# Decoding float64 weights on the chip: clearing the sign on ScalarE, and two decodes in every unit of the second stage

## The chip, the core and the metric

One core of a Trainium2 chip runs the whole program. The metric is the device time of one execution in microseconds (us). TensorE does the matrix products, VectorE and ScalarE the elementwise work and all reads of TensorE's output (PSUM), POOL (GpSimd) elementwise work between SBUF tiles, and SP issues the transfers. In views of the profile they are PE, DVE, ACT, POOL and SP; PEld is TensorE's loading of weights.

## What is computed

```python
def reference(**kwargs):
    ...
    attn_out = _attn_ref(**attn_kwargs)      # local causal attention plus a memory term, 4 x 8 heads, 576 x 64
    x = np.ascontiguousarray(attn_out.transpose(0, 2, 1, 3)).reshape(B * S, H * D)   # 2304 x 512
    x = _moe_ref(x=x, **moe_kwargs)
    return _moe2_ref(x=x, **moe2_kwargs)

def _moe_ref(x, w_in, w_out):                # 512 -> 2048 -> 512
    h = x @ w_in
    sp = np.where(h > 20.0, h, np.log1p(np.exp(np.minimum(h, 20.0))))
    g = h * np.tanh(sp)
    return (g @ w_out).astype(np.float32)

def _moe2_ref(x, w1, w2, w3, w_out):         # 512 -> 1024 -> 512
    a = x @ w1
    b = x @ w2
    h = a * b @ w3
    return (h @ w_out).astype(np.float32)
```

The weights come as float64, so each number is two 32-bit words in memory. The kernel builds each value out of the words and splits it into a rounded part and a remainder, for three products in place of one.

## The kernel before

The program has three stages. **Attention** goes over 16 pairs of heads. The **second stage** is `_moe_ref`: the 2048 hidden columns come in four quarters, and each quarter goes over eight units (four batches, `b`, by two halves, `z`, of 288 rows). In a unit `emit_h` makes the hidden values: 48 matmuls, then tanh, arctan and sine on ScalarE with two loads of its function table (L471, L474), a product on VectorE (L482), and the split into `gh` (ScalarE, L485) and `gl` (VectorE, L65). `emit_x2` multiplies them with the second weights: 48 matmuls into X banks of PSUM, which VectorE empties into `x2` (L575 in the first quarter, L577 later). It runs one unit behind `emit_h`. The **third stage** is `_moe2_ref`; w3 and the last weights are multiplied with each other (`fold`) during the last quarter and the start of the third stage.

`decode` turns a block of 128 x 512 weights into floats: a transfer of the raw words (`draw`, L92), six operations on VectorE (L98 to L104) and an addition on POOL (L105). `split_w` then rounds and subtracts on POOL into the weight tile `wqt` (L62, L65). `split_to_dram`, used by `predecode` for the weights of the third stage, does the same in place (L62, L120) and writes both parts to DRAM (L121, L122). The buffers `da`, `de` and `draw` exist once in attention and twice in the second stage, so a decode can't start until POOL, or a write, is done with an earlier one.

What is decoded when is set by generators: `steps(gen, n)` takes n blocks from one. Attention takes ten blocks. In the second stage `nextq` loads the eight blocks of the next quarter and `pre` the 22 blocks of the third stage that are left. The framework then orders each engine's instructions by its own simulated schedule, so their order is not that of the code; an engine works off its instructions in the order given to it.

Of the kernel before, what the change touches and what calls it, by code (L numbers as in the profile page):

```python
# [9 lines left out]
F32 = mybir.dt.float32  # L10
# [3 lines left out]
AF = mybir.ActivationFunctionType  # L14
ALU = mybir.AluOpType
# [6 lines left out]
def fused_kernel(ctx: ExitStack, tc, q, k, v, M_prev, z_prev, beta, w_in, w_out, w1, w2, w3, w_out2, out):  # L22
    nc = tc.nc
# [31 lines left out]
    def f(ap):  # L55
        return ap.bitcast(F32)
# [13 lines left out]
    def steps(gen, n):  # L70

        for _ in range(n):
            next(gen, None)
# [9 lines left out]
    def decoder(stack, raw, n):  # L83
        dec.update(pool=stack.enter_context(tc.tile_pool(name="dec", bufs=1)), raw=raw, n=n)

    def dec_tile(tag):
        return dec["pool"].tile([128, WN], F32, tag=tag, name=tag, bufs=dec["n"])

    def decode(src):

        r = dec["pool"].tile([128, WN, 2], I32, tag="draw", name="draw", bufs=dec["raw"])
        dm(out=r.rearrange("p n t -> p (n t)"), in_=src)  # L92
        lw, hw = r[:, :, 0], r[:, :, 1]
        a = dec_tile("da")
        e = dec_tile("de")
        ai, ei = a.bitcast(I32), e.bitcast(I32)
        V = nc.vector
        V.tensor_scalar(out=ai, in0=hw, scalar1=0x7FFFFFFF, scalar2=None, op0=ALU.bitwise_and)  # L98
        V.tensor_scalar(out=a, in0=a, scalar1=2.0 ** -15, scalar2=122879.9921875, op0=ALU.max, op1=ALU.min)  # L99
        V.tensor_scalar(out=ai, in0=ai, scalar1=3, scalar2=0x3FFFFFF8,  # L100
                        op0=ALU.logical_shift_left, op1=ALU.bitwise_and)
        V.scalar_tensor_tensor(out=ai, in0=hw, scalar=-0x40000000, in1=ai, op0=ALU.bitwise_and, op1=ALU.bitwise_or)  # L102
        V.tensor_scalar(out=ei, in0=ai, scalar1=-0x800000, scalar2=None, op0=ALU.bitwise_and)  # L103
        V.scalar_tensor_tensor(out=e, in0=lw.bitcast(U32), scalar=2.0 ** -52, in1=e, op0=ALU.mult, op1=ALU.mult)  # L104
        nc.gpsimd.tensor_tensor(out=a, in0=a, in1=e, op=ALU.add)  # L105
        return a, e
# [4 lines left out]
    def split_w(hi, lo, src):  # L111
        a, _ = decode(src)
        pool_round(hi, a)
        sub(lo, a, hi, nc.gpsimd)

    def split_to_dram(dst, src):

        a, e = decode(src)
        pool_round(e.bitcast(F32R), a)
        nc.gpsimd.tensor_tensor(out=a.bitcast(F32R), in0=a, in1=e, op=ALU.subtract)  # L120
        dm(out=dst[0], in_=e)  # L121
        dm(out=dst[1], in_=a)  # L122
# [16 lines left out]
    def predecode():  # L139
        for w, wd in ((w1, w1_dram), (w2, w2_dram), (w_out2, o2_dram)):  # L140
            for c in range(w.shape[0] // 128):
                for h in range(w.shape[1] // WN):
                    split_to_dram(wd[:, 128 * c:128 * c + 128, WN * h:WN * h + WN], words(w, 128 * c, WN * h))
                    yield
# [13 lines left out]
    def load_quarter(g):  # L158
        t = (wq if g % 2 == 0 else w2q[0]).tile([128, 2, KD + KQ, FQ], F32R, tag=f"wq{g % 2}", name="wqt")
        wts[g] = t  # L160
        for c in range(KD):
            split_w(t[:, 0, c], t[:, 1, c], words(w_in, 128 * c, FQ * g))
            yield
        for c in range(KQ):
            split_w(t[:, 0, KD + c], t[:, 1, KD + c], words(w_out, FQ * g + 128 * c, 0))
            yield
# [16 lines left out]
        out=mask, in_=mask, pattern=[[-1, 512]], compare_op=ALU.is_ge,  # L183
# [4 lines left out]
    for hv in (UP, DN):  # L188
        nc.gpsimd.affine_select(
            out=mask4[hv], in_=mask4[hv], pattern=[[-1, CH]], compare_op=ALU.is_ge,  # L190
# [263 lines left out]
    def emit_h(u):  # L454

        g, b, z = u
        t = wts[g]
        x = xl[b]
        cs = slice(CH * z, CH * z + CH)
        y = [wps[0].tile([128, 2, CH], F32, tag=f"y{i}", name="y", bufs=1) for i in range(2)]  # L460
        hp = []
        for m in range(KQ):
            o = bank(HU.get(u, HT[g == NQ - 1])[m])[:, 0:CH]
            ms = slice(128 * m, 128 * m + 128)
            for kk in range(KD):
                mm(o, t[:, 0, kk, ms], x[:, 0, kk, cs], kk == 0, False)
                mm(o, t[:, 0, kk, ms], x[:, 1, kk, cs], False, False)
                mm(o, t[:, 1, kk, ms], x[:, 0, kk, cs], False, kk == KD - 1)
            hp.append(o)
        for m in range(KQ):  # L470
            nc.scalar.activation(out=y[m // 2][:, m % 2], in_=hp[m], func=AF.Tanh, scale=0.5)  # L471

        d = wps[0].tile([128, 1], F32, tag="dum", name="dum", bufs=2)
        first = nc.scalar.activation(out=d, in_=y[1][:, 1, 0:1], func=AF.Sin, scale=0.0)  # L474
        with tc.issue_after(first.ins):
            for i in range(2):
                nc.scalar.activation(out=y[i], in_=y[i], func=AF.Arctan, scale=-0.5, bias=half)
        gg = []
        for i in range(2):
            nc.scalar.activation(out=y[i], in_=y[i], func=AF.Sin, scale=-2.0, bias=halfpi)  # L480
            for j in range(2):
                nc.vector.tensor_tensor(out=y[i][:, j], in0=y[i][:, j], in1=hp[2 * i + j], op=ALU.mult)  # L482
            gh = wps[0].tile([128, 2, CH], F32R, tag="gh", name="gh", bufs=3)
            gl = wps[0].tile([128, 2, CH], F32R, tag="gl", name="gl", bufs=3)
            nc.scalar.copy(out=gh, in_=y[i])  # L485
            sub(gl, y[i], gh)
            gg.append((gh, gl))
        gt[u] = gg
# [9 lines left out]
    pre = predecode()  # L498
# [61 lines left out]
    def emit_x2(u):  # L560
        g, b, z = u
        t = wts[g]
        gg = gt.pop(u)
        c0 = S * b + CH * z
        for m in range(KD):
            o = psX()[:, 0:CH]
            ms = slice(128 * m, 128 * m + 128)
            for kk in range(KQ):
                gh, gl = (x[:, kk % 2] for x in gg[kk // 2])
                mm(o, t[:, 0, KD + kk, ms], gh, kk == 0, False)  # L570
                mm(o, t[:, 1, KD + kk, ms], gh, False, False)
                mm(o, t[:, 0, KD + kk, ms], gl, False, kk == KQ - 1)
            d = x2[:, m, c0:c0 + CH]
            if g == 0:
                nc.vector.tensor_copy(out=d, in_=o)  # L575
            else:
                nc.vector.tensor_tensor(out=d, in0=d, in1=o, op=ALU.add)  # L577
# [37 lines left out]
    def from_dram(t, d, cols):  # L615
        for i in range(2):
            dm(out=f(t[:, i]), in_=d[i, :, cols].rearrange("(k p) f -> p k f", p=128))

    def w_slot(s, name):
        return xp.tile([128, 2, KD, 512], F32R, tag=f"xs{s}", name=name, padded_shape=[128, 2, KD, S])  # L620

    folding = fold()
    nextq = iter(())
    prev = None
    w1t, w2t, wft = [None, None], [None, None], [None]
    for u in [(g, b, z) for g in range(NQ) for b in range(B) for z in range(2)]:
        g, b, z = u
        last = g == NQ - 1
        if u not in gt:
            if last and fpool[0] is None:  # L630
                steps(nextq, 100)
                steps(pre, 100)
                dk.close()
                fpool[0] = fk.enter_context(tc.tile_pool(name="fp", bufs=1))
                decoder(fk, 1, 2)
            emit_h(u)
        if last:
            if z == 0 and b > 0:
                wt, wd = ((w1t, w1_dram), (w2t, w2_dram))[(b - 1) % 2]
                i = (b - 1) // 2  # L640
                wt[i] = w_slot(b - 1, "w12t")
                from_dram(wt[i], wd, slice(512 * i, 512 * i + 512))
            if b > 0:
                steps(folding, 3)
        if prev is not None:
            emit_x2(prev)
        if not last:
            if b == 0 and z == 0:
                nextq = load_quarter(g + 1)
            steps(nextq, 2)  # L650
            steps(pre, 1)
        prev = u
    emit_x2(prev)
    w2t[1] = w_slot(3, "w12t")
# [53 lines left out]
    for c in range(NC):  # L708
        emit_ab(c)
        if c == 1:  # L710
# [4 lines left out]
            for i in range(2):  # L715
                for s in range(2):
                    dm(
                        out=f(wft[0][:, i, 4 * s:4 * s + 4]),
                        in_=w_dram[i, 512 * s:512 * s + 512, :].rearrange("(k p) f -> p k f", p=128),
# [36 lines left out]
```

## Time and profile before

| | |
|---|---|
| median of the runs before | 1073.4 us (1073.21 to 1075.92, 3 runs) |
| the profiled execution | 1075.49 us, with a span of 1073.7 us from the first to the last instruction |
| TensorE, matmuls | 1023.7 us busy, 95% of the span |
| VectorE | 671.9 us, 63% |
| ScalarE | 548.0 us, 51% |
| POOL | 387.3 us, 36% |
| granted TensorE clock | 0.991 of full speed on average |
| attention, second stage, third stage | about 0 to 285 us, 285 to 720 us, the rest; they overlap at the ends |

Busy shares are means over stages that differ, so they are to be read by stretch. A row's "idle before" is time in which that engine stood still, with what released it.

### The profile page before, as it was taken

The page shows a single profiled execution, that of the slowest core. Times are in us where ns is not written, and L with a number is a line of the kernel's source. Part 1 is how long each engine was busy: PE and PEld are TensorE (multiplying, and loading weights), DVE is VectorE, ACT ScalarE, POOL GpSimd, SP SyncE. Part 2 cuts the span into 40 slices and gives each one's busy share as a digit, 9 for nine tenths or more (in the row PEclk, how much of TensorE's full clock was granted, in tenths as well). Part 3 has the DMA queues.
Part 4 walks back from the last instruction along what each step waited for, and adds up shares of the span by engine and source line. Part 5 has one row for each costly group of instructions (what it writes and reads, how often), then busy time and mean ns, then how long its engine had stood idle before and what let it go on. Part 6 is the DMA issues. An engine that isn't in the chain of part 4 may idle for free.

```text
span 1073.7 us, 19071 instructions
## 1 busy us (share of the span) xinstructions
PE 1023.7 (95%) x7128; PEld 913.2 (85%) x7128; DVE 671.9 (63%) x1563; ACT 548.0 (51%) x1157; POOL 387.3 (36%) x377
## 2 busy tenths in 40 slices
PE   6998898899998999999999999999999999999998
PEld 5665655567798999999999999999998999999997
DVE  6699999896689888888987535647551122222220
ACT  5776767677765666666666655653231222222221
POOL 7668898784255556555555001010100000000000
PEclk9999999999999999999999999999999999999999
DMA  6788777675233343333332264323115100000001
GB/s 149 167 188 188 186 181 184 169 187 117 79 98 101 112 161 109 109 130 127 118 99 101 63 243 146 136 89 128 62 58 176 40 5 17 20 21 16 6 20 40
DMA packets 111341, 116.70 MB, mean 109 GB/s; under 512 B 71696, under 2 KB 73744, under 8 KB 111248
## 3 DMA queue, kind: packets, MB, share of 16 engines
q1 hardware_dynamic: 111248, 115.48, 37.6%
q8 instruction: 56, 0.92, 0.4%
q14 instruction: 37, 0.30, 0.1%
HBM read 71.83 MB, written 21.50 MB: 87 GB/s over the span
## 4 chain that ended last, share of the span: by engine, by line
PE 62%; DVE 20%; POOL 7%; DMA 6%; issue 3%; SPq 1%; ACT 0%; DVEq 0%; POOLq 0%; ACTq 0%
PE psA L59 28%; PE psX L59 24%; PE psF L59 6%; DVE de L104 3%; POOL da L120 2%; DVE da L102 2%; PE psF L426 2%; DVE de L103 2%; DVE s L361 2%; DVE da L99 2%; POOL da L105 2%; DVE da L98 2%; DVE da L100 2%; DMA w_dram<-da 1%; DVE s L356 1%
## 5 line engine op out<-in xcount | busy, mean ns | idle before, releaser
L105 POOL TENSOR_TENSOR da<-da,de 128x512 f32<-128x512 f32 x72 | 100.1, 1395 | 336.0 <-DVE de L104 272.6
L59 PE MATMUL psX<-gh,wqt 128*128 128x288 f32 x1024 | 209.0, 298 | 9.9 <-DVE x L575 5.4
L59 PE MATMUL psA<-x2h,w12t 128*128 128x256 f32 x1152 | 210.4, 283 | 0.0
L59 PEld LDWEIGHTS psA<-x2h,w12t 128*128 128x128 f32 x1152 | 180.8, 192 | 1.0
L59 PEld LDWEIGHTS psX<-gh,wqt 128*128 128x128 f32 x1024 | 164.6, 188 | 13.5 <-DVE x L575 6.7
L59 PE MATMUL psA<-x2l,w12t 128*128 128x256 f32 x576 | 163.2, 284 | 0.4 <-DVE x2l L65 0.4
L59 PE MATMUL psX<-gl,wqt 128*128 128x288 f32 x512 | 150.9, 295 | 0.0
L686 DVE TENSOR_TENSOR bs<-bs,psA 128x256 f32<-128x256 f32 x72 | 30.3, 421 | 161.5 <-PE psA L59 156.8
L59 PE MATMUL psA<-xt,wqt 128*128 128x288 f32 x840 | 119.9, 296 | 0.0
L59 PEld LDWEIGHTS psA<-xt,wqt 128*128 128x128 f32 x840 | 115.0, 189 | 2.3 <-issue 1.0
L59 PEld LDWEIGHTS psA<-x2l,w12t 128*128 128x128 f32 x576 | 110.3, 192 | 1.4 <-DVE x2l L65 0.7
L366 ACT ACTIVATE s<-s,acc 128x512 f32<-128x512 f32 (+4 forms) x144 | 84.2, 587 | 39.7 <-DVE acc L361 34.2
L59 PE MATMUL psX<-wft,pbuf 128*128 128x512 f32 x432 | 101.7, 394 | 2.3 <-DMA wft<-w_dram 2.3
L59 PEld LDWEIGHTS psX<-wft,pbuf 128*128 128x128 f32 x432 | 81.4, 190 | 19.3 <-DMA wft<-w_dram 2.8
L59 PEld LDWEIGHTS psX<-gl,wqt 128*128 128x128 f32 x512 | 96.5, 189 | 0.2
L687 ACT CAST pbuf<-bs 128x256 fp32r<-128x256 f32 x72 | 29.3, 406 | 110.4 <-DVE bs L686 97.3
L98 DVE TENSOR_SCALAR da<-draw 128x512 int32<-128x512 int32 x72 | 44.1, 616 | 61.5 <-DMA draw<-in_moe_w_dram 23.1
L59 PE MATMUL psF<-xt,wqt 128*128 128x288 f32 x552 | 77.3, 295 | 0.0
L426 PE MATMUL psF<-ident,s 128*128 128x128 f32 x400 | 67.7, 283 | 10.0 <-DVE s L356 6.6
L59 PE MATMUL psX<-pt,raw 128*64 128x64 f32 (+4 forms) x576 | 74.8, 329 | 0.0
L59 PEld LDWEIGHTS psF<-xt,wqt 128*128 128x128 f32 x552 | 74.5, 188 | 0.1
L361 DVE CUSTOM_DVE_ANT_0 s<-psA,mask 128x512 f32<-128x512 f32 (+3 forms) x144 | 64.2, 477 | 15.0 <-PE psA L59 11.0
(116 smaller groups left out, 1920.8 us busy)
## 6 DMA issues: line engine op xcount, KB each, us to landing
draw<-in_moe_w_dram SPq DMA_DIRECT2D x32, 512.0 KB, 3.7
draw<-in_moe_w_out_dram SPq DMA_DIRECT2D x24, 512.0 KB, 3.9
draw<-in_moe_w_in_dram SPq DMA_DIRECT2D x16, 512.0 KB, 4.4
w12t<-w_dram SPq DMA_DIRECT2D x8, 1024.0 KB, 7.8
w_dram<-de SPq DMA_DIRECT2D x24, 256.0 KB, 2.4
w_dram<-da SPq DMA_DIRECT2D x24, 256.0 KB, 2.4
out_dram<-ob SPq DMA_DIRECT2D x18, 256.0 KB, 2.0
eqk<-hl SPq DMA_DIRECT2D x30, 144.0 KB, 2.7
```

The lines of the kernel that those rows point to most:

```text
L59: nc.tensor.matmul(o, lhsT=l, rhs=r, start=start, stop=stop)
L98: V.tensor_scalar(out=ai, in0=hw, scalar1=0x7FFFFFFF, scalar2=None, op0=ALU.bitwise_and)
L99: V.tensor_scalar(out=a, in0=a, scalar1=2.0 ** -15, scalar2=122879.9921875, op0=ALU.max, op1=ALU.min)
L100: V.tensor_scalar(out=ai, in0=ai, scalar1=3, scalar2=0x3FFFFFF8, op0=ALU.logical_shift_left, op1=ALU.bitwise_and)
L102: V.scalar_tensor_tensor(out=ai, in0=hw, scalar=-0x40000000, in1=ai, op0=ALU.bitwise_and, op1=ALU.bitwise_or)
L104: V.scalar_tensor_tensor(out=e, in0=lw.bitcast(U32), scalar=2.0 ** -52, in1=e, op0=ALU.mult, op1=ALU.mult)
L105: nc.gpsimd.tensor_tensor(out=a, in0=a, in1=e, op=ALU.add)
L361: nc.vector.tensor_tensor_reduce(out=s, in0=o, in1=m, op0=ALU.add, op1=ALU.min, scale=-scale, scalar=init, accum_out=a,)
L366: nc.scalar.activation(out=s, in_=s, func=AF.Exp, scale=-1.0, bias=a, accum_out=r)
L426: nc.tensor.transpose(o[:, 128 * x:128 * x + 128], src[:, 128 * jb:128 * jb + 128], ident)
L686: nc.vector.tensor_tensor(out=bs, in0=bs, in1=pa, op=ALU.mult)
L687: nc.scalar.copy(out=t[:, 0, m], in_=bs)
```

## The change

Two edits. The first of the six VectorE operations of a decode, which cleared the sign bit of the high word by a bitwise and, becomes an absolute value of the same word, read as a float, on ScalarE. And the numbers of blocks that a unit of the second stage takes change: before, two from `nextq` (until its eight are used up, in the first four units) and one from `pre` in each unit; after, a table of eight pairs, which adds up to eight of `nextq` and seven of `pre` per quarter.

```diff
-        V.tensor_scalar(out=ai, in0=hw, scalar1=0x7FFFFFFF, scalar2=None, op0=ALU.bitwise_and)
+        nc.scalar.activation(out=a, in_=r.bitcast(F32)[:, :, 1], func=AF.Abs)
         V.tensor_scalar(out=a, in0=a, scalar1=2.0 ** -15, scalar2=122879.9921875, op0=ALU.max, op1=ALU.min)
...
             if b == 0 and z == 0:
                 nextq = load_quarter(g + 1)
-            steps(nextq, 2)
-            steps(pre, 1)
+
+            nq, npre = ((1, 1), (2, 0), (1, 1), (1, 1), (1, 1), (1, 1), (1, 1), (0, 1))[2 * b + z]
+            steps(nextq, nq)
+            steps(pre, npre)
```

The order of the instructions moves in three places that matter here. First ScalarE at the start of the second stage, from the last evacuation of attention (L447) to the second table load of the unit that follows it. Before:

```order
L428 COPY pt<-psF 128x128
L447 CAST xt_3220<-psX 128x512
L447 CAST xt_3220<-psX 128x64
L471 ACT_TABLE_LOAD
L471 ACTIVATE y<-psF 128x288
L471 ACTIVATE y<-psX 128x288
L471 ACTIVATE y<-psF 128x288
L471 ACTIVATE y<-psX 128x288
L474 ACT_TABLE_LOAD
```

After:

```order
L428 COPY pt<-psF 128x128
L98 ACTIVATE da<-draw 128x512
L447 CAST xt_3220<-psX 128x512
L447 CAST xt_3220<-psX 128x64
L471 ACT_TABLE_LOAD
L471 ACTIVATE y<-psF 128x288
L98 ACTIVATE da<-draw 128x512
L471 ACTIVATE y<-psX 128x288
L471 ACTIVATE y<-psF 128x288
L471 ACTIVATE y<-psX 128x288
L98 ACTIVATE da<-draw 128x512
L474 ACT_TABLE_LOAD
```

Three of the new operations stand in the row: ahead of the evacuation, among the tanh, and ahead of the table load.

Next ScalarE in a unit in the middle of the second quarter, from the sines (L480) to the tanh of the next unit (L471). Before:

```order
L480 ACTIVATE y<-y,halfpi 128x576 x2
L485 CAST gh<-y 128x576 x2
L471 ACT_TABLE_LOAD
L471 ACTIVATE y<-psA 128x288 x2
L471 ACTIVATE y<-psF 128x288 x2
```

After:

```order
L480 ACTIVATE y<-y,halfpi 128x576 x2
L485 CAST gh<-y 128x576
L98 ACTIVATE da<-draw 128x512
L485 CAST gh<-y 128x576
L98 ACTIVATE da<-draw 128x512
L471 ACT_TABLE_LOAD
L471 ACTIVATE y<-psA 128x288 x2
```

One new operation stands between the two casts, one behind them.

Last VectorE in such a unit, from the first `gl` (L65) to the first evacuation of the next product (L577). Before:

```order
L65 TENSOR_TENSOR gl<-y,gh 128x576
L577 TENSOR_TENSOR x_3941<-x_3941,psX 128x288
L98 TENSOR_SCALAR da<-draw 128x512
L65 TENSOR_TENSOR gl<-y,gh 128x576
L577 TENSOR_TENSOR x_3941<-x_3941,psX 128x288
L99 TENSOR_SCALAR da<-da 128x512
L100 TENSOR_SCALAR da<-da 128x512
L98 TENSOR_SCALAR da<-draw 128x512
L102 SCALAR_TENSOR_TENSOR da<-draw,da 128x512
L99 TENSOR_SCALAR da<-da 128x512
```

After:

```order
L65 TENSOR_TENSOR gl<-y,gh 128x576
L577 TENSOR_TENSOR x_3941<-x_3941,psX 128x288
L99 TENSOR_SCALAR da<-da 128x512
L577 TENSOR_TENSOR x_3941<-x_3941,psX 128x288
L100 TENSOR_SCALAR da<-da 128x512
L65 TENSOR_TENSOR gl<-y,gh 128x576
L99 TENSOR_SCALAR da<-da 128x512
L102 SCALAR_TENSOR_TENSOR da<-draw,da 128x512
L100 TENSOR_SCALAR da<-da 128x512
L103 TENSOR_SCALAR de<-da 128x512
```

L98 is gone from VectorE, and each L99 now needs a result of ScalarE; the second `gl` comes one operation later. ScalarE's table loads (ACT_TABLE_LOAD) number 64 in both orders.

## Rows read from the trace of the kernel before

**Rows 1.** The page's first part: busy us, share of the span, instructions.
```profile
PE 1023.7 (95%) x7128; PEld 913.2 (85%) x7128; DVE 671.9 (63%) x1563; ACT 548.0 (51%) x1157; POOL 387.3 (36%) x377
```

**Rows 2.** Stretches: their length, each engine's busy us, clock, DMA share, GB/s.
```profile
0.00:90.00 90.00, 74.61 (x455) 52.27 (x455) 65.94 (x196) 57.09 (x156) 60.41 (x79) 0.98 0.75 170
90.00:240.00 150.00, 131.76 (x857) 87.78 (x857) 140.14 (x391) 102.27 (x295) 124.33 (x126) 0.98 0.76 182
240.00:285.00 45.00, 44.94 (x330) 33.93 (x329) 31.16 (x117) 32.16 (x93) 15.28 (x20) 1.00 0.41 99
285.00:400.00 115.00, 109.50 (x811) 104.80 (x810) 97.39 (x182) 73.84 (x117) 59.49 (x50) 1.00 0.35 111
400.00:505.00 105.00, 103.64 (x775) 102.77 (x774) 90.67 (x179) 67.79 (x105) 58.47 (x49) 1.00 0.37 123
505.00:612.00 107.00, 103.94 (x768) 103.24 (x767) 83.21 (x166) 67.41 (x106) 51.11 (x43) 0.98 0.31 101
```

**Rows 3.** TensorE's waits from 285 to 612 us: total, times, longest.
```profile
PE psX L59 <- DVE x L575: 5.4, 4, 2.3
PE psX L59 <- DVE x L577: 4.3, 4, 2.1
```

**Rows 4.** Stretches for line 98 alone: VectorE's busy us in it.
```profile
0.00:90.00 90.00, 2.05 (x2) 0.98 0.75 170
90.00:240.00 150.00, 4.46 (x8) 0.98 0.76 182
285.00:612.00 327.00, 30.79 (x46) 0.99 0.34 112
```

**Rows 5.** The chain of waits from 285 to 400 us, shares by line.
```profile
by line: PE psX L59 10.2%; DMA w_dram<-da 9.5%; DVE de L104 8.4%; issue 8.0%; POOL da L120 7.5%; DVE de L103 6.6%; DVE da L102 6.4%; DVE da L99 5.9%; DVE da L98 5.9%; DVE da L100 4.3%; POOL da L105 3.8%; DVE x L575 3.5%; POOL de L62 3.1%; P
```

**Rows 6.** VectorE's waits from 285 to 612 us, those at L98.
```profile
DVE da L98 <- POOL wqt L65: 18.0, 12, 2.2
DVE da L98 <- DMA w_dram<-da: 12.0, 9, 2.5
DVE da L98 <- DMA draw<-in_moe_w_dram: 8.7, 2, 7.2
...
DVE da L98 <- DMA o_dram<-da: 3.8, 4, 1.7
```

**Rows 7.** Groups of ScalarE by shape: busy us, mean ns, idle before.
```profile
L485 ACT CAST gh<-y 128x576 fp32r<-128x576 f32 x64 | 43.2, 675 | 53.4 <-DVE y L482 39.9 <-PE psX L59 11.3 <-DVE da L100 2.2
...
L447 ACT CAST xt<-psX 128x512 fp32r<-128x512 f32 x16 | 9.3, 580 | 4.7 <-PE psX L59 4.5
```

**Rows 8.** VectorE in order of time, 470 to 478 us: start, duration.
```profile
471.40 0.43 DVE L98 TENSOR_SCALAR da<-draw 128x512 int32<-128x512 int32 x1 [0.82 <-DMA w_dram<-da]
...
476.11 0.98 DVE L104 SCALAR_TENSOR_TENSOR de<-draw,de 128x512 f32<-128x512 uint32 x1
477.02 0.44 DVE L577 TENSOR_TENSOR x<-x,psX 128x288 f32<-128x288 f32 x1
```

**Rows 9.** TensorE in order of time, 462 to 480 us.
```profile
471.40 0.43 PE L59 MATMUL psX<-gh,wqt 128*128 128x288 f32 x2
...
477.51 0.54 PE L59 MATMUL psX<-gh,wqt 128*128 128x288 f32 x2 [1.15 <-DVE x L577]
```

**Rows 10.** ScalarE in order of time, 463 to 465 us.
```profile
463.75 0.67 ACT L485 CAST gh<-y 128x576 fp32r<-128x576 f32 x1 [0.27 <-DVE y L482]
```

**Rows 11.** POOL in order of time, 463 to 469 us.
```profile
467.17 1.29 POOL L120 TENSOR_TENSOR da<-da,de 128x512 fp32r<-128x512 f32 x1
```

**Rows 12.** VectorE in order of time, at the second stage's start.
```profile
298.00 1.49 DVE L98 TENSOR_SCALAR da<-draw 128x512 int32<-128x512 int32 x1 [2.19 <-POOL wqt L65]
```

**Rows 13.** ScalarE in order of time, at the second stage's start.
```profile
295.58 1.28 ACT L471 ACT_TABLE_LOAD   x1
```

**Rows 14.** VectorE in order of time, at the last quarter's start.
```profile
593.13 0.43 DVE L98 TENSOR_SCALAR da<-draw 128x512 int32<-128x512 int32 x1 [7.16 <-DMA draw<-in_moe_w_dram]
```

**Rows 15.** TensorE in order of time, at the last quarter's start.
```profile
596.81 0.53 PE L59 MATMUL psX<-gh,wqt 128*128 128x288 f32 x2 [2.06 <-DVE x L577]
```

## The prediction

> **What bounds the kernel now.** I read the profile's head first: TensorE is busy for 95% of the span [rows 1], so only its holes and the stages where another engine paces it can give time back. The table by stretches comes next. From 90 to 240 us (attention) VectorE is busy for 140.1 of 150 us and TensorE for 131.8: VectorE paces it. From 240 to 285 TensorE works 44.9 of 45 us, so nothing is to be had there. From 285 to 612 (the second stage) TensorE works 109.5, 103.6 and 103.9 of 115, 105 and 107 us [rows 2]. What it waited for in these 327 us has two entries only: VectorE's two evacuations of an X bank, L575 (5.4 us) and L577 (4.3 us), 9.7 us in eight waits [rows 3]. That is all that the second stage can gain. A unit there is 96 matmuls; 103.64 us by 775 is 134 ns each, 12.8 us a unit, while 105 us hold 775/96 = 8.1 units, 13.0 us each [rows 2].
>
> The chain of waits says why VectorE is late. Between 285 and 400 us it runs around the decode loop itself: L98 to L104 on VectorE, the POOL operations, and the write to w_dram that frees the buffer [rows 5]. VectorE stands at L98 for 42.5 us in the second stage, for a buffer that POOL (18.0) or a write (12.0 and 3.8) has not freed, or for the raw weights (8.7) [rows 6]. One such unit: the second L98 begins at 471.40 after a wait of 0.82, the last L104 ends at 477.09, and only then L577 runs [rows 8]; TensorE, wanting its bank from 476.36, starts at 477.51 [rows 9].
>
> **The change, part by part.** *What leaves VectorE.* Ten decodes lie in attention: two L98 before 90 us (2.05 us) and eight from 90 to 240 (4.46 us) [rows 4]. In the latter stretch VectorE is busy for 93%, so I count 0.93 x 4.46 = 4.2 us; before 90 us it is busy for 65.9 of 90 us [rows 2] and I count half, 1.0. Bounds: 0 (another wait follows each time) and 6.5.
>
> *What ScalarE gets.* No ScalarE row reads every second word. The nearest that go from SBUF to SBUF are 675 ns for 576 columns; out of PSUM 580 ns for 512 [rows 7]. I take 0.6 us (675 x 512/576). As an upper bound I take twice that, 1.2 us, as if the words skipped cost as much as those read; as a lower one 0.42, what VectorE needed in a quiet place [rows 8]. L98's mean in the second stage is 30.79/46 = 0.67 us [rows 4], so the operation costs about the same on either engine. In attention ScalarE is busy 102 of 150 us [rows 2]; ten operations queue ahead of exponentials and casts that VectorE and TensorE want, and L99 now waits for another engine. For that I charge 0.2 us each, 2 us; bounds 0 and 6 (ten times 0.6). Attention: -5.2 + 2 = about -3 us.
>
> [...]
>
> *The second stage, middle of a quarter.* Before, L98 holds VectorE; now the Abs stands in ScalarE's queue, between the two gh casts or just behind them. If POOL is not done, what waits behind it is the second gh cast, then gl, then the table load and the tanh of the next unit. In the unit around 464 us the first gh cast starts at 463.75 [rows 10] and POOL's last operation ends at 468.46 [rows 11], 4.7 us later. An Abs that waits so long moves the second cast to about 469.1 to 469.8 and gl to 470.5. The output product that reads them starts at 471.40 [rows 9] and needs them after its first 0.8 us, at 472.2: 1.7 us to spare. VectorE's side: in the trace the last L104 ended 5.7 us after the second L98 began. Second Abs at 5.3 us behind the first gh cast, 0.6 us long, then 5.3 us (5.7 without the L98): 11.2 us behind the cast; TensorE wants the bank at 476.36, 12.6 us behind it [rows 9]. So the waits of this kind vanish when the schedule holds.
>
> *The even spread.* The order table shows two decodes per unit before too: the two buffers had paced them already. What the new counts change is who follows whom. Before, a quarter ends in units with two predecodes, both of which hold their buffers until a write has landed; after, each unit has one of either kind, and one unit per quarter a single decode, in which a lag is recovered. One predecode is left for the start of the last quarter.
>
> *Start of the stage.* Here the change costs. In the new order an Abs stands in ScalarE ahead of the last attention evacuation and the first table load, and a further one ahead of the next table load. In the trace L98 at this place began at 298.00, released by POOL [rows 12], while ScalarE's table load started at 295.58 [rows 13]. Behind the Abs and the two casts the load comes at about 298.0 + 0.6 + 0.8 = 299.4, some 3.9 us later. The output product of that unit was already tight, and I charge 3 us of new TensorE wait (bounds: 0 and 8, the latter if the second of these Abs adds as much again).
>
> *Last quarter.* L98 of the first w3 block waited 7.16 us for its weights [rows 14], and TensorE then lost 2.06 us [rows 15]. These weights wait for the last predecode's write, so the wait moves to ScalarE; I keep the 2.06. From 612 us on ScalarE takes 14 more operations, 8 us in all, under a TensorE without holes: nothing.
>
> Second stage: -(9.7 - 2.1 - 3.0) = -4.6. **Sum**: -3 - 4.6 = -7.6 us. The profiled execution took 1075.5 us (its span of 1073.7 and 1.8 around it), 2.1 above the median of 1073.4; it would take 1067.9. Against the median: 1065.8, said as **1066**.
>
> **Rivals.** *Full gain.* No wait at the start or at w3, and all of L98's time in attention: -9.7 - 6.5 = -16, 1057 us. For it: VectorE at 93%. Against it: the Abs ahead of the table load.
>
> *It cancels.* ScalarE hands over late in attention, so that nothing is won there, and the start costs its 8 us: -9.7 + 2.1 + 8 = 0.4, with a few us either way 1071 to 1076. For it: the chain between 285 and 400 runs round a loop whose length the change hardly alters (0.67 for 0.6).
>
> *Slower: the decode loop paces ScalarE and so TensorE.* If the two handovers and 0.18 us more per Abs (0.6 for 0.42) lengthen the loop of two decodes, a unit follows it: gh, tanh and the next product are late by the same amount in every unit. With 0.35 to 1 us per unit over some 20 units that is 7 to 20 us; with 0.5 us, the waits of [rows 3] kept and attention's 3 us gained, it is 7 us more than now, 1080. It decides once the Abs comes more than about 1.7 us later behind the gh cast than the 4.7 us read above. Against it: one light unit per quarter, in which the lag is made good.
>
> **How the numbers follow.** A measurement of this kernel tells about 0.3% (3.2 us) from no change. Forecast (1061 to 1070): 0.46. Full gain (under 1061): 0.15. Cancels (1070 to 1076.5): 0.23. Slower (over 1076.5): 0.16. The cases under 1070.2 make 0.61 faster, 0.23 the same, 0.16 slower. The range leaves out the best part of the full gain and the longer half of the slower case: 1057 to 1078.
>
> **What would show it.** Right: L98 gone from VectorE and about 72 ScalarE operations of 0.6 us on draw; VectorE's busy time from 90 to 240 us lower by some 4 us and that stretch shorter by 2 to 4; TensorE's waits for L575 and L577 down to about half, with none above 1 us in the second and third quarter; a new wait of 2 to 4 us shortly after the stage starts; the waits of [rows 6] found again at ScalarE's L98, some 40 us of them. Wrong: Abs much longer than 0.6 us; attention as long as before; TensorE waiting for gh or gl (ScalarE's cast late) in every unit; ScalarE's tanh late, so that the A and F banks hold up the first product.

## The result and the profile after

The changed kernel takes 1086.8 us (median of 4 runs, 1084.87 to 1089.51), beside 1074.1 us for the kernel before (4 runs, 1073.21 to 1075.92; the 1073.4 us given above is the median of three of them): a ratio of 1.0118, 95% interval [1.0089, 1.0147]. It is slower by 1.2%, outside the predicted range. The profiled execution took 1089.5 us, with a span of 1087.7 us.

The head of the page and the new line of ScalarE:

```profile
span 1087.7 us, 19198 instructions
...
PE 1030.0 (95%) x7128; PEld 917.5 (84%) x7128; DVE 650.1 (60%) x1491; ACT 585.4 (54%) x1229; POOL 379.2 (35%) x377
...
L98 ACT ACTIVATE da<-draw 128x512 f32<-128x512 f32 x72 | 48.1, 673 | 79.9 <-POOL wqt L65 36.2
```

The span grew by 14.0 us. TensorE spends 7.7 us more of it without a matmul (1087.7 - 1030.0 = 57.7, before 1073.7 - 1023.7 = 50.0 [rows 1]) and 6.3 us more on the same 7128 matmuls. The same work in more time points to a lower clock (0.986 granted on average, before 0.991), so two things have to be found, holes and clock.

The stretches of [rows 2], for the changed kernel (the column behind POOL is the clock):

```profile
0.00:90.00 90.00, 74.27 (x429) 52.16 (x430) 61.60 (x187) 57.44 (x155) 59.08 (x78) 0.96 0.72 164
90.00:240.00 150.00, 130.78 (x855) 86.85 (x854) 139.85 (x375) 103.04 (x294) 116.05 (x122) 0.97 0.75 178
240.00:285.00 45.00, 44.75 (x313) 32.73 (x311) 32.31 (x121) 34.63 (x102) 20.00 (x25) 1.00 0.47 110
285.00:400.00 115.00, 110.56 (x831) 106.04 (x831) 96.91 (x169) 82.46 (x135) 58.77 (x50) 1.00 0.36 121
400.00:505.00 105.00, 104.22 (x784) 103.98 (x783) 81.39 (x156) 75.45 (x123) 53.55 (x46) 1.00 0.36 112
505.00:612.00 107.00, 104.25 (x783) 103.67 (x781) 79.24 (x155) 76.32 (x124) 51.73 (x44) 1.00 0.32 103
```

By 285 us TensorE has done 1597 matmuls, before 1642: attention is slower. From 285 to 612 us it does more than before in each row (831, 784 and 783 for 811, 775 and 768), 44 in all, and has caught up. In attention the clock stands at 0.96 and 0.97, for 0.98 twice; by the rows that is at most 0.04 x 90 + 0.03 x 150 = 8.1 us lost to the clock, where it was 0.02 x 240 = 4.8 (at most, since TensorE is not busy throughout). VectorE is busy 139.85 us from 90 to 240, for 140.14, so the 4 us that were to leave it are not seen as free time. Over the whole span, too, VectorE's busy time fell by 21.8 us only (671.9 [rows 1] to 650.1), though the 72 operations that left it had taken 44.1: `gl` (L65) now takes 1013 ns for 911 and L100 526 for 448, and no run here shows why. ScalarE's first table load of the second unit, at 295.58 before [rows 13], now starts at 300.99; 0.67 of these 5.4 us is the Abs ahead of it.

Next the waits from 285 to 612 us, TensorE's, those of ScalarE at the new line and VectorE's for it:

```profile
PE psX L59 <- DVE x L575: 3.2, 3, 1.5
PE psX L59 <- DVE x L577: 1.1, 2, 0.8
PE psX L59 <- DVE gl L65: 0.7, 1, 0.7
PE psF L59 <- DVE y L482: 0.6, 1, 0.6
```

```profile
ACT da L98 <- POOL wqt L65: 36.2, 17, 3.5
ACT da L98 <- DMA w_dram<-da: 13.7, 8, 3.2
...
ACT da L98 <- DMA o_dram<-da: 8.6, 4, 3.5
```

```profile
DVE da L99 <- ACT da L98: 42.2, 24, 3.6
```

The 9.7 us of [rows 3] have become 5.6, and 2.5 more at 612.06, just behind this stretch, for the first w3 block, whose wait before [rows 15] lay inside it: 8.1 in all. The waits of [rows 6] stand at ScalarE, 58.5 us in the three rows where some 40 were forecast, with VectorE 42.2 us behind it. The stage gains, if less than forecast.

Since as many matmuls are done by 612 us as before, the 14 us are lost behind that. First the stretch from there until TensorE has nothing left but the products with `wft`, the folded weights, for the kernel before and for the kernel after:

```profile
612.00:816.50 204.50, 204.05 (x1451) 195.35 (x1450) 111.14 (x226) 89.41 (x154) 18.21 (x14) 1.00 0.36 121
```

```profile
612.00:823.20 211.20, 207.73 (x1452) 197.53 (x1452) 105.30 (x216) 97.77 (x169) 19.98 (x15) 0.99 0.33 113
```

For the same matmuls TensorE needs 6.7 us more. Short waits are 3.0 of them (3.5 us for 0.5), and the clock, 0.94 from 612 to 640 us, is 1.7; the other 2.0 stay open. The rest of the loss is one load, and the clock behind it. TensorE in order of time, from the end of the fold, and SP's queue at the same place:

```profile
828.25 1.65 PE L59 MATMUL psX<-wft,pbuf 128*128 128x512 f32 x3 [5.01 <-DMA wft<-w_dram]
831.93 10.44 PE L59 MATMUL psX<-wft,pbuf 128*128 128x512 f32 x32 [2.04 <-DMA wft<-w_dram]
```

```profile
822.68 0.92 SPq L719 DMA_DIRECT2D wft<-w_dram  x2
823.70 0.45 SPq L611 DMA_DIRECT2D w_dram<-da  x1
...
832.53 0.98 SPq L719 DMA_DIRECT2D wft<-w_dram  x2
```

The folded weights are loaded into `wft`, a buffer that the fold still reads (as `o2`), so that SP can issue the load only when the last w3 block is multiplied, at 822.68. TensorE has run out of other work by 823.2 and waits for 5.01 and 2.04 us. Before, SP issued the load at 810.63, TensorE had other work until 816.55, and the wait came to 2.3 us in all:

```profile
810.63 0.92 SPq L717 DMA_DIRECT2D wft<-w_dram  x2
```

```profile
816.55 0.86 PE L59 MATMUL psX<-wft,pbuf 128*128 128x512 f32 x3
819.75 9.20 PE L59 MATMUL psX<-wft,pbuf 128*128 128x512 f32 x33 [2.35 <-DMA wft<-w_dram]
```

Behind the hole the clock falls. Stretches of 10 us, for the kernel after and for the kernel before:

```profile
820.00:830.00 10.00, 4.89 (x22) 3.46 (x20) 1.83 (x2) 0.59 (x1) 0.00 (x0) 0.89 0.58 177
830.00:840.00 10.00, 8.06 (x23) 6.37 (x24) 1.18 (x3) 1.64 (x5) 0.00 (x0) 0.59 0.80 293
```

```profile
810.00:820.00 10.00, 7.65 (x58) 7.10 (x57) 2.25 (x3) 0.86 (x2) 0.00 (x0) 0.97 0.77 257
820.00:830.00 10.00, 10.00 (x42) 8.28 (x43) 1.61 (x4) 1.87 (x5) 0.00 (x0) 0.86 0.62 215
830.00:840.00 10.00, 10.00 (x66) 9.07 (x65) 1.55 (x4) 2.26 (x5) 0.00 (x0) 1.00 0.15 54
```

At 0.89 and 0.59 the 20 us of the first fence lose 5.2 us to the clock (0.11 x 10 + 0.41 x 10), around a wait of 7.0 us; before, 0.97 and 0.86 lost 1.7 us, around a wait of 2.3 us. The longer wait and the lower clock are together at most 8.2 us of the 14, since a low clock costs nothing while TensorE stands; the stretch ahead of them is the other part.

### The profile page after: what moved, and what is told of

Read it like the earlier page. It is cut to its first block, busy times and chain, and to the rows that moved or that the text cites. A ratio compares the mean times of both kernels' runs of the same rounds, so it can differ in the third digit from the quotient of the medians.

```text
span 1087.7 us, 19198 instructions
## 1 busy us (share of the span) xinstructions
PE 1030.0 (95%) x7128; PEld 917.5 (84%) x7128; DVE 650.1 (60%) x1491; ACT 585.4 (54%) x1229; POOL 379.2 (35%) x377
## 4 chain that ended last, share of the span: by engine, by line
PE 60%; DVE 18%; DMA 7%; POOL 6%; issue 4%; ACT 3%; SPq 1%; ACTq 0%; POOLq 0%; DVEq 0%
PE psA L59 27%; PE psX L59 23%; PE psF L59 6%; PE psF L426 3%; DVE de L104 2%; DVE s L356 2%; DVE da L99 2%; POOL da L105 2%; DVE da L102 2%; DVE de L103 2%; POOL da L120 2%; DVE s L361 2%; DMA draw<-in_moe_w_dram 1%; PE psX L262 1%; DVE da L100 1%
## 5 line engine op out<-in xcount | busy, mean ns | idle before, releaser
L105 POOL TENSOR_TENSOR da<-da,de 128x512 f32<-128x512 f32 x72 | 98.3, 1368 | 347.1 <-DVE de L104 272.0
L98 ACT ACTIVATE da<-draw 128x512 f32<-128x512 f32 x72 | 48.1, 673 | 79.9 <-POOL wqt L65 36.2
L59 PE MATMUL psX<-pt,raw 128*64 128x64 f32 (+4 forms) x576 | 77.1, 333 | 0.0
```

What stands on the lines that cost most here:

```text
L59: nc.tensor.matmul(o, lhsT=l, rhs=r, start=start, stop=stop)
L98: nc.scalar.activation(out=a, in_=r.bitcast(F32)[:, :, 1], func=AF.Abs)
```

## The experiments

In what follows "place" is the number of matmuls that stand, in the order given to TensorE, ahead of the transposes (L597) of the last w3 block. The first product with `wft` always has place 5116. (The traces list 320 records more ahead of either, so that the distance between the two is the same there.) The place is 5018 in the kernel before and 5064 after: the framework's order puts the end of the fold 46 matmuls later, and these are missing as cover for the load. The experiments carry a switch for each of the three decoders; it moves the lines behind it by three, so that L575 and L577 are L578 and L580 there.

```diff
-        nc.scalar.activation(out=a, in_=r.bitcast(F32)[:, :, 1], func=AF.Abs)
+        if dec["act"]:
+            nc.scalar.activation(out=a, in_=r.bitcast(F32)[:, :, 1], func=AF.Abs)
+        else:
+            V.tensor_scalar(out=ai, in0=hw, scalar1=0x7FFFFFFF, scalar2=None, op0=ALU.bitwise_and)
```

**Which edit costs (e1 to e4).** The diffs of e1 to e4 are against the changed kernel with all three switches at True; "old spread" is the code of before.

*e1, the even spread alone.*
```diff
-    decoder(at, 1, 1, True)
+    decoder(at, 1, 1, False)
...
-    decoder(dk, 2, 2, True)
+    decoder(dk, 2, 2, False)
...
-                decoder(fk, 1, 2, True)
+                decoder(fk, 1, 2, False)
```


> The even spread alone, with the sign cleared on VectorE everywhere as before. Theory A (the absolute value costs, wherever a decode stands alone and its six operations are one chain: attention about 5 us, fold about 10 us): 1068 to 1074 us, attention as before (last qd matmul near 275 us), fold as before. Theory B (the spread costs: TensorE's order of the fold depends on when the last predecode is taken, and its last w3 block stands some 50 matmuls later than before in that order): about 1080 us, attention as before, TensorE waiting 5 to 7 us for wft as in the changed kernel.

*e2, the Abs alone, in all three decoders.*
```diff
-            nq, npre = ((1, 1), (2, 0), (1, 1), (1, 1), (1, 1), (1, 1), (1, 1), (0, 1))[2 * b + z]
-            steps(nextq, nq)
-            steps(pre, npre)
+            steps(nextq, 2)
+            steps(pre, 1)
```


> The absolute value on ScalarE in all three decoders, with the old spread. Theory A: about 1085 us (attention +5, fold +10, the second stage a little under 0). Theory B: 1076 to 1080 us (attention +5, no wait of TensorE for wft beyond some 3 us).

*e3, even spread, Abs in the second stage only.*
```diff
-    decoder(at, 1, 1, True)
+    decoder(at, 1, 1, False)
...
-                decoder(fk, 1, 2, True)
+                decoder(fk, 1, 2, False)
```


> Even spread, and the absolute value on ScalarE only in the second stage's decoder (48 of the 72 decodes or so); attention and fold clear the sign on VectorE. Theory A: 1067 to 1071 us, faster than before by the waits on L575 and L577 that go. Theory B: about 1076 us, since the fold is late in TensorE's order all the same; attention as before under both.

*e4, the changed kernel with the fold back on VectorE.*
```diff
-                decoder(fk, 1, 2, True)
+                decoder(fk, 1, 2, False)
```


> The changed kernel with the fold alone back on VectorE. Theory A: about 1077 us (10 less than the changed kernel), TensorE's wait for wft near 2 us. Theory B: 1084 to 1087 us, no better than the changed kernel within 0.3%, wait for wft 5 to 7 us.

| kernel | median us | ratio to before, 95% interval | place | wait for wft, us |
|---|---|---|---|---|
| e1, spread alone | 1084.60 | 1.0107 [1.0083, 1.0132] | 5071 | 7.5 |
| e2, Abs alone | 1079.45 | 1.0051 [1.0032, 1.0070] | 5047 | 5.5 |
| e3, spread, Abs in second stage | 1082.55 | 1.0080 [1.0059, 1.0100] | 5071 | 7.6 |
| e4, spread, Abs in attention and second stage | 1084.25 | 1.0097 [1.0078, 1.0115] | 5071 | 7.4 |

The kernel before, on the same chip, took 1073.83 us. Both edits cost, the spread more: +10.8 us. Theory A, which blamed the Abs alone, falls with e1; B holds there for the wait, but its numbers came out too low: e1 and e3 took 4.6 and some 6.5 us more than it gave, and in e2 TensorE waits 5.5 us for `wft` where it allowed some 3. From e1 the sum goes on step by step: -2.1 with the Abs in the second stage (e3), +1.7 with attention's (e4), +2.6 with the fold's (the changed kernel, 1086.8, on another chip). The intervals of each two neighbours overlap, so that none of these three steps is told apart from nothing here.

**One number of the table, and one decoder at a time (e5 to e8).** Theory C laid the place to the single block of the third stage that the new table leaves over.

*e5, as e1, but none left over.*
```diff
-            nq, npre = ((1, 1), (2, 0), (1, 1), (1, 1), (1, 1), (1, 1), (1, 1), (0, 1))[2 * b + z]
+            nq, npre = ((1, 1), (2, 0), (1, 1), (1, 1), (1, 1), (1, 1), (1, 1), (0, 2))[2 * b + z]
```


> The even spread alone (sign cleared on VectorE), with one number of the table changed: the eighth unit of a quarter takes two predecodes for one, so that none of the 22 is left for the start of the last quarter. Theory C (the cost of the spread is this one block that is left over: it moves the fold's last w3 block from place 5018 to 5071 among TensorE's matmuls, while the first product with wft stays at place 5116, so that the load of wft, which waits for the fold, is no longer covered): the last block is at 5018 again, TensorE's wait for wft at 2 to 3 us, and the time 1071 to 1075 us, 10 less than with the even spread alone (1084.6). Theory D (spreading itself costs, by the decodes in every unit): 1080 us or more, with the lost time between 285 and 720 us.

*e6, e7 and e8, the kernel before (its switches at False) with the Abs in the second stage, the fold or attention only.*
```diff
-    decoder(dk, 2, 2, False)
+    decoder(dk, 2, 2, True)
```


> The absolute value on ScalarE in the second stage's decoder alone, old spread; fold and attention as before. TensorE's order has the last w3 block at place 5018. Theory C with a gain of the second stage: 1069 to 1073 us (the same 2 us that it gave under the even spread, up to the 4.6 forecast). Theory E (nothing is gained there, since the decode loop is no shorter): 1074 within 0.3%.


```diff
-                decoder(fk, 1, 2, False)
+                decoder(fk, 1, 2, True)
```


> The absolute value on ScalarE in the fold's decoder alone, old spread. TensorE's order has the last w3 block at place 5047, 29 matmuls later than before. Theory C (place in TensorE's order decides): 1076 to 1079 us, wait for wft 4 to 5.5 us, nothing lost before 700 us. Theory F (a wait of the fold's chain for ScalarE costs, not the order): the fold's casts fall behind block by block from 640 us on, and TensorE waits for w3h or for POOL's result.


```diff
-    decoder(at, 1, 1, False)
+    decoder(at, 1, 1, True)
```


> The absolute value on ScalarE in attention's decoder alone (ten decodes), old spread. From the changed kernel, where attention ended 4.7 us later: 1077 to 1079 us, the first table load of the second stage near 290 us for 286.0. If attention's loss there was chance of one execution: 1074 within 0.3%. If the forecast of 3 us gained holds: 1071.

| kernel | median us | ratio to before, 95% interval | place | wait for wft, us |
|---|---|---|---|---|
| e5, even spread, none left over | 1088.40 | 1.0143 [1.0120, 1.0166] | 5018 | 2.3 |
| e6, Abs in second stage | 1070.83 | 0.9974 [0.9962, 0.9985] | 5018 | 2.2 |
| e7, Abs in fold | 1081.39 | 1.0074 [1.0050, 1.0097] | 5047 | 5.3 |
| e8, Abs in attention | 1077.35 | 1.0035 [1.0017, 1.0053] | 5018 | 2.3 |

In e5 the place and the wait for `wft` are those of before, as C has it, and yet the kernel has the highest median of all: its loss lies in the second stage. TensorE's waits there:

```profile
PE psX L59 <- DVE x L580: 13.2, 9, 2.2
PE psX L59 <- DVE x L578: 5.8, 3, 3.2
```

That is 19.0 us for 9.7 in [rows 3]. So the table sets two things at once, the place of the fold and the waits for X banks, and C's sum fails. E falls: the second stage alone gains (e6). F falls too: in e7 the fold's casts of its products, of which the first comes at 637.5 us and the fourth at 713.1, are no later than before (641.7 and 716.5), and in its profile the loss comes at the end, in the wait for `wft`. That profile is of the fastest of six runs (1076.8); the median of 1081.4 lies above the 1076 to 1079 us that C gave, and no profile shows those 4.6 us.

In e8 TensorE's time without matmuls fell by about what was forecast, from 50.0 to 46.5 us (1076.1 - 1029.6), but its matmuls took 1029.6 us for 1023.7, at a granted clock of 0.986 for 0.991. Two rows show how a hole arises. TensorE of e8, and VectorE just before:

```profile
206.26 1.13 PE L59 MATMUL psX<-phi,mr 128*128 128x512 f32 x2 [2.42 <-DVE xt L65]
```

```profile
202.99 1.54 DVE L102 TENSOR_SCALAR da<-da 128x512 f32<-128x512 f32 x1
204.57 0.77 DVE L103 TENSOR_SCALAR da<-da 128x512 int32<-128x512 int32 x1
...
205.38 0.69 DVE L105 SCALAR_TENSOR_TENSOR da<-draw,da 128x512 int32<-128x512 int32 x1
205.99 0.22 DVE L65 TENSOR_TENSOR xt<-psX,xt 128x64 fp32r<-128x64 f32 x1
```

L102, L103 and L105 are L99, L100 and L102 of the changed kernel. Three operations of a decode stand ahead of the small evacuation (L65, `xt`) that frees TensorE's bank. At this place the kernel before has the large and the small evacuation at 203.45 and 204.47 us, with one decode operation between them, and TensorE waited 1.20 us. That such holes are what lowers the clock in attention is argued from this place and not shown: from 0 to 285 us TensorE is busy for 254.9 us in e8 and for 251.3 before, so in sum its holes there are shorter.

**The table again (e9 to e12).**

*e9, the kernel before with one block of the third stage left over.*
```diff
-            steps(nextq, 2)
-            steps(pre, 1)
+            nq, npre = ((2, 1), (2, 0), (2, 1), (2, 1), (0, 1), (0, 1), (0, 1), (0, 1))[2 * b + z]
+            steps(nextq, nq)
+            steps(pre, npre)
```


> Sign cleared on VectorE. The blocks of the next quarter as before (two in each of the first four units), but seven of the third stage's blocks per quarter, so that one of the 22 is left for the start of the last quarter, as in the changed kernel; TensorE's order has the last w3 block at place 5018 nevertheless. Theory G (the block left over is itself what delays the fold): about 1082 us, wait for wft 5 to 7.5 us. Theory H (the place of the fold in TensorE's order decides, whatever is left over): wait for wft 2 to 3 us, 1072 to 1077 us.

*e10, as e1, but none left over and no unit with two blocks of the third stage.*
```diff
-            nq, npre = ((1, 1), (2, 0), (1, 1), (1, 1), (1, 1), (1, 1), (1, 1), (0, 1))[2 * b + z]
+            nq, npre = ((1, 1), (2, 1), (1, 1), (1, 1), (1, 1), (1, 1), (1, 1), (0, 1))[2 * b + z]
```


> Sign cleared on VectorE, even spread, all 22 blocks taken in time (eight per quarter: the second unit takes two of the next quarter and one of the third stage, the eighth takes one alone). Last w3 block at place 5018. Theory H: wait for wft 2 to 3 us. Theory I (the 11 us that the even spread with a double eighth unit lost in the second stage came from that unit, just ahead of the quarter's change): 1073 to 1077 us. Theory J (they came from three decodes' worth of work that is never followed by a light unit): 1080 us or more, waits on X banks of 10 us or more.

*e11 and e12, the tables of e10 and of e9 with the Abs in the second stage.*
```diff
-    decoder(dk, 2, 2, False)
+    decoder(dk, 2, 2, True)
```


> The same table with eight per quarter, and the absolute value on ScalarE in the second stage's decoder alone. If H and I hold and the second stage gains its 2 to 3 us: 1069 to 1074 us. If J: 1077 or more.

> Old spread of the next quarter's blocks, seven of the third stage's per quarter, and the absolute value on ScalarE in the second stage's decoder alone. H: 1069 to 1073 us, as with the old spread (1070.8). G: about 1079 us.

| kernel | median us | ratio to before, 95% interval | X-bank waits, us |
|---|---|---|---|
| e9 | 1077.99 | 1.0045 [1.0029, 1.0061] | 12.0 |
| e10 | 1081.07 | 1.0060 [1.0038, 1.0083] | 12.3 |
| e11, e10 with Abs | 1074.26 | 1.0003 [0.9986, 1.0019] | 7.9 |
| e12, e9 with Abs | 1064.56 | 0.9913 [0.9896, 0.9931] | 2.8 |

The place is 5018 in all four and the wait for `wft` 2.2 or 2.3 us, so G falls: a block left over does not delay the fold by itself, nor does the even spread by itself (e10); with the sign cleared on VectorE only both together did. H holds for that wait, though e9's time came out 1.0 us above what it gave, with X-bank waits of 12.0 us. J, not I, holds for e10, though by J e11 should have taken 1077 us or more. And e12 beats both kernels, and by 4.4 us its own expectation; the kernel before took 1074.51 us on the same chip. Its waits of TensorE, to be set beside [rows 3]:

```profile
PE psX L59 <- DMA wft<-w_dram: 2.3, 1, 2.3
PE psX L59 <- DVE x L578: 2.0, 3, 1.4
PE psX L59 <- DVE x L580: 0.8, 2, 0.4
```

Against the kernel before it has two differences: the Abs in the second stage, and seven blocks of the third stage in each quarter for eight, eight and six, so that the second unit of a quarter has two decodes and not three. The first alone gains 3.2 us (e6), the second alone costs 3.5 (e9), and both together gain 10.

**The same kernel, one thing at a time (e13 to e15).** All three start from e12.

*e13, only the fold later.*
```diff
-                steps(folding, 3)
+                steps(folding, 1 + (b > 1))
```


> The kernel with the absolute value in the second stage alone, the old spread of the next quarter's blocks and seven of the third stage's per quarter (1064.6 us), with the fold alone taken later: two units of the last quarter take two of its steps for three. Every engine's row is the same up to the first w3 block; the last w3 block then stands at place 5071 in TensorE's row for 5018. Theory H (place decides): TensorE's wait for wft 7 to 8 us for 2.3, the clock down behind it, 1070 to 1075 us. Rival (the place is only a sign of something earlier): 1063 to 1067 us.

*e14 and e15, the Abs in the fold's decoder too, and in attention's too.*
```diff
-                decoder(fk, 1, 2, False)
+                decoder(fk, 1, 2, True)
```


> The same 1064.6 us kernel with the absolute value also in the fold's decoder; rows the same up to the first w3 block, last w3 block at place 5047. Theory H: wait for wft 5.3 to 5.5 us, 1068 to 1071 us. Forecast's step (nothing, since ScalarE has room there): 1063 to 1066 us.


```diff
-    decoder(at, 1, 1, False)
+    decoder(at, 1, 1, True)
```


> The same 1064.6 us kernel with the absolute value also in attention's decoder; fold on VectorE, last w3 block at place 5018. Theory K (in attention the absolute value moves decode work on VectorE ahead of evacuations that TensorE waits for, and TensorE's clock falls more often behind such holes): 1067 to 1070 us, five or six dips of the clock before 290 us for the four of the 1064.6 us kernel. Forecast's step (3 us gained): 1061 to 1063 us.

| kernel | median us | ratio to before, 95% interval | place | wait for wft, us |
|---|---|---|---|---|
| e13, fold later | 1075.92 | 1.0013 [0.9991, 1.0034] | 5071 | 8.1 |
| e14, Abs in the fold | 1071.23 | 0.9973 [0.9954, 0.9991] | 5047 | 5.6 |
| e15, Abs in attention | 1065.89 | 0.9923 [0.9895, 0.9951] | 5018 | 2.6 |

In e13 the two units of the second batch in the last quarter take one step of the fold for three, the four behind them two (the expectation speaks of two units; the edit slows six). Every engine's order is that of e12 up to the first w3 block, in the traces up to 639 us, the sign is cleared on the same engines, and 11.4 us are lost (10.7 by the two ratios, which were taken on different chips). TensorE and the stretch in which it waits, in e13:

```profile
813.83 1.65 PE L59 MATMUL psX<-wft,pbuf 128*128 128x512 f32 x3 [5.87 <-DMA wft<-w_dram]
817.68 10.91 PE L59 MATMUL psX<-wft,pbuf 128*128 128x512 f32 x36 [2.21 <-DMA wft<-w_dram]
```

```profile
810.00:820.00 10.00, 3.96 (x9) 2.67 (x10) 0.00 (x0) 0.00 (x0) 0.00 (x0) 0.64 0.76 255
820.00:830.00 10.00, 10.00 (x41) 8.16 (x40) 1.61 (x4) 1.76 (x5) 0.00 (x0) 0.85 0.54 204
```

The hole and the clock are those of the changed kernel. This settles H: the place is a cause, not a sign of one. (A buffer of its own for `wft`, which would take the wait away and leave the place, was not run.) e14 loses 6.7 us (6.4) at place 5047, in proportion: 29 of 53 places is 0.55, 6.7 of 11.4 us 0.59. Both times lie just above H's ranges, by 0.9 and 0.2 us. e15 stands 1.3 us above e12 with intervals that overlap, so its time shows neither the forecast's 3 us nor K's loss. Its profile speaks for K: the clock is lower from 60 to 150 us, and the second stage's first load at L474 (L477 in these kernels) starts at 290.2 us, in e12 at 286.8. The stretch in e15, and then in e12:

```profile
60.00:150.00 90.00, 77.38 (x467) 50.37 (x465) 78.11 (x204) 58.04 (x161) 64.57 (x68) 0.92 0.77 175
```

```profile
60.00:150.00 90.00, 77.75 (x500) 51.53 (x498) 82.89 (x229) 59.16 (x172) 70.89 (x72) 0.96 0.82 186
```

The clock reads 0.92 and 0.96. Over all profiles this load starts at 286.2 to 290.7 us where attention has the Abs (e2, e4, e8, e15 and the changed kernel) and at 283.8 to 287.0 in the twelve where it has not. The clock from 0 to 285 us keeps the two apart: 0.96 or 0.97 in the five, 0.98 or 0.99 in the twelve.

## Why the prediction was wrong

**The sum.** It gave -7.6 us, and 12.7 were measured the other way. Term by term, by e1, e3, e4 and the changed kernel: the even spread 10.8 for 0, the second stage -2.1 for -4.6, attention 1.7 for -3, the fold 2.6 for 0. Only the first is clear of the noise in that row; for the others the experiments from the kernel before and from e12 decide.

**What bounds the kernel.** That the X-bank waits of [rows 3] are all that the second stage can gain was wrong. Four pairs differ in the Abs of the second stage alone. Before and e6: 2.2 us less waiting (9.7 to 7.5), 3.2 us less time. e1 and e3: 1.4 (7.9 to 6.5) and 2.1, the latter within the noise. e10 and e11: 4.4 and 6.8. e9 and e12: 9.2 and 13.4. Each time the gain is about one and a half times the wait in the profile. That the rest is TensorE's clock is borne out by the last pair, whose clock from 285 to 612 us reads 0.986 with the wait (e9, the mean of its stretches of 2 us) and 1.00 without (e12): as an estimate 0.014 x 327 = 4.6 us, beside the 4.2 that are left (13.4 - 9.2). In the smaller pairs, too, the clock of 285 to 612 us reads 0.01 higher with the Abs (1.00 for 0.99, and 0.99 for 0.98 in e11), but with one profile each that is too few to tell.

**The Abs in the second stage.** Right in sign and mechanism: -2.1 (e3), -3.2 (e6), -6.8 (e11) and -13.4 us (e12), by the table that it stands beside, for the forecast's -4.6. Its duration was taken as 0.6 and came out as 0.673, while L98 on VectorE averaged 0.616 over its 72. By these two durations alone the move loses 0.06 us an operation; by the time it gains, since it is VectorE's queue that TensorE waits for here (9.7 us in [rows 3]).

**Start of the stage.** About as charged: the table load came 5.4 us later where 3.9 was read, and after it TensorE waits 1.55 and 1.08 us for L575, 0.68 for `gl` and 0.59 for L482, 3.9 us in place of the 3 charged. The w3 wait, kept at 2.06, was 2.48.

**Attention, "-3".** Failed: it cost 3.3 us in e8, 1.7 in e4 against e3, and 1.3 in e15, this last not told apart from nothing. In e8's profile TensorE's holes shrank by 3.5 us over the whole span, and 5.9 went to the clock. That the clock falls in attention was in the rows, 0.98 in [rows 2], and I gave it no term.

**The even spread.** This is the largest failure. The step saw that one predecode is left for the last quarter and that each quarter has a light unit, and gave the two no price. The spread alone cost 10.8 us. By the profiles of e1 and of the kernel before, 5.2 us of that is the wait for `wft` (7.5 for 2.3), and the clock behind it fell to 0.55 from 820 to 830 us. What the spread did was to move the end of the fold 53 places later in TensorE's order, from 5018 to 5071, so that the load behind it lost its cover.

**"From 612 us on ... under a TensorE without holes: nothing."** Failed, and the first cause of the failure above. TensorE had no hole there because the end of the fold was just covered: the wait of 2.3 us for `wft` was in the trace of before, as the only sign that a load is the limit at that point. I asked whether the 14 operations fit into ScalarE's free time, and not whether they or the spread move the end of the fold in TensorE's order. All seventeen kernels line up by place: 5018 has 2.2 to 2.6 us of wait, 5047 5.3 to 5.6, 5064 7.0, 5071 7.4 to 8.1. In the fold the Abs alone cost 7.3 us (e7) and 6.7 (e14).

**The rivals.** None was the case. The slower one (the decode loop paces each unit) has the right size by chance: the time lies in its band and its waits are there, 42.2 us at L99, but TensorE did not follow them.

**What stays open.** Why the framework's schedule sets the end of the fold later when the even spread and a block left over come together; why the X-bank waits differ as they do between tables (7.9, 12.0, 12.3 and 19.0 us with the sign cleared on VectorE); why the Abs in the second stage gains 13.4 us beside the table of e9 and 3.2 beside that of before; and whether the fold's Abs costs anything on top of the even spread (2.6 us, within the noise, and the place, 5064 for 5071, gives no reason for a loss).

## What to carry to other kernels

Where a framework orders the instructions, a change of counts or of an engine in one stage moves work in stages that it does not touch: compare the places of the last producer and of the first consumer of every load that has just enough cover. Here a wait of 2.3 us for a DMA, in a stage without other waits of TensorE above 0.4 us, marked such a load. Take an edit apart by stage before it is judged: here the same Abs gained in one stage and cost in two, and the version that keeps it in the gaining stage alone takes 1070.8 us, with the table of e12 1064.6.

## What the runs showed of the hardware

A hole in TensorE was paid for twice. Behind a wait of 7 to 8 us for `wft` the granted clock read 0.55 (e1), 0.59 (the changed kernel) or 0.64 (e13) over 10 us; these differ by where the stretches are cut, and in stretches of 2 us it reads 0.50 for 8 to 10 us on end in all three (822 to 830, 828 to 838, 814 to 822). The changed kernel:

```profile
828.00:838.00 10.00, 7.71 (x17) 5.62 (x18) 0.04 (x1) 0.40 (x1) 0.00 (x0) 0.50 0.79 277
```

In this stretch TensorE spent 0.45 us on each of 17 matmuls of 128x512 (7.71 us); from 850 to 1080 us, at a clock of 1.00, it spent 0.23 us on each of 356 (82.0 us).

Behind a short hole the clock fell or did not: after a wait of 2.2 or 2.3 us it read 0.86 in the kernel before and stayed at 1.00 in e6, e11 and e12. What decides it is not shown here.

On ScalarE an Abs that reads every second word took 673 ns for 512 columns, and a cast of 576 adjacent columns 675 ns [rows 7], 600 for 512 in proportion: as an estimate, the skipped words cost about an eighth, not as much again as the prediction's upper bound allowed for.
